# A gated recurrence with two products behind it: first products in pairs of blocks, and an opening that runs the recurrence ahead

## The chip, the cores and the metric

The kernel runs on one core of a Trainium2 chip. The metric is the device time of one execution in microseconds (us). The runs of the kernel before gave 195.75, 196.1 and 196.6 us, so the median is 196.1. One execution was also recorded by the hardware profiler, with all instructions of the engines: TensorE (PE, with its weight loads as PEld), VectorE (DVE), ScalarE (ACT), GpSimd (POOL) and SyncE (SP), which issues most transfers.

## The reference

```python
B, H, S, D = 4, 8, 768, 48
for t in range(S):
    state = alpha[:, :, t, :, None] * state + np.einsum('bhd,bhe->bhde', k[:, :, t], v[:, :, t])
    y[:, :, t] = np.einsum('bhd,bhde->bhe', q[:, :, t], state)
x = y.transpose(0, 2, 1, 3).reshape(B * S, H * D)      # 3072 x 384
h = x @ w_in                                           # 384 x 2048
r = np.maximum(h, 0.0)
g = s * (r * r) + b
out = g @ w_out                                        # 2048 x 384
```

For each of the 4 x 8 heads a state of 48 x 48 decays by alpha and takes in k and v, step by step in time; q reads it. The 8 heads of a step side by side are a row of 384, which goes through two matrix products with a squared Relu between them.

## The kernel before, in words

The 3072 rows are 24 blocks of 128 steps, six to each of the four sequences. For a block n the recurrence is computed in chunk form. In the order of its parts, with the names in the code:

- `load(n)`: four transfers of 192 KB each (alpha, k, q, v) into rings of eight buffers, issued by SP.
- `ln(n)`: ACT takes the logarithm of alpha. `vcast(n)`: POOL casts v.
- `cum(n)`: PE sums the logarithms over time (L210, for the first five blocks also the totals, L213) into the bank ct_ps; ACT takes exp(-) and exp(+) of it, bi_sb and b_sb (L221, L222). From the sixth block on, `decay(n)` writes the last row of b_sb to memory and reads it back transposed into blast, on SP (L230, L232); the second transfer waits for the landing of the first. The last block of a sequence has none.
- `qk(n)`: DVE multiplies k by bi_sb and q by b_sb (L238, L239). `tr(n)`: eight PE transposes into ct_ps (L244), copied by DVE to qkT (L249).
- `amat(n)`: eight small products q.k (L259) into the two banks a_ps, masked by DVE into am_a and am_b (L267).
- `y(n)`: products with the state of the block before and with the masked scores into y_ps (L278, L287), the products for the new state (L298), ACT's copy to y_bf (L305), and the new state by DVE (t_sb, L334) and POOL (L339, L343).
- `xt(n)`: three PE transposes of y_bf into an h_ps bank (L312), copied by ACT into xd_all (L318).

Behind it stand the two products. `m(n, u)`, u from 0 to 3, is a unit of the first: it fills one bank h_ps of 512 columns with four groups of three products of 128 columns (L365), ACT takes the Relu into r_sb (L379), DVE squares it into gt_all (L386). Two banks h_ps alternate, and xt uses them too. `o(n, u)`, u from 0 to 3, is a quarter of the second: four products of 384 columns (L402) into o_ps, or for blocks 1 and 2 into the two a_ps (`o_in_a`). After the last quarter the bank is evicted: for blocks 0 to 13 by ACT into room that the cast of w_in has freed (`keep_sb`, L411), for later ones by DVE with the bias (L415) and a store. `last(u)` is the second product of block 23, in two halves of 192 columns (L425).

Nothing schedules this at run time. Every engine runs its instructions in the order in which the program issues them, and the program sorts a list of events by a hand-given position. The opening, blocks 0 to 3 and part of 4, is one list written out (position 0.1 times its index). There w_in is cast while it lands (`win`), w_out in four parts (`wout`: parts 0, 1 and 3 by DVE in whole or in part, 2 by ACT), the column sums of w_out for the bias are built (`colsum`), and `busy` puts filler products. Behind it a block takes eight units of position: for block n, p = 8n is where y(n) stands; ln, cum, qk, tr, amat come up to 16.7 units ahead of it, xt one unit after, m(n, u) at p + 2.5 to 7.5 and o(n, u) at p + 8.5 to 14.5. `load(n + 5)` stands at p - 2.5. `GROUPS` gives how many blocks share a first product; here it is one for all.

Of the kernel before, what the change touches and what calls it, by code (L numbers as in the profile page):

```python
# [10 lines left out]
AF = mybir.ActivationFunctionType  # L11
# [3 lines left out]
def kernel(  # L15
# [12 lines left out]
    nc = tc.nc  # L28

    B, H, S, D = q.shape  # L30
    C = 128
    NCH = S // C
    NP = H // 2
    NBLK = B * NCH
    d_model = moe_w_in.shape[0]
# [1 line left out]
    NJ = d_ff // 128  # L37
    KT = d_model // 128

    GROUPS = [1] * NBLK  # L40
    UNITS = 5
    assert sum(GROUPS) == NBLK
    NLD = 8

# [10 lines left out]
    a_ps = [ps.tile([128, NP, 128], FP32, name=f"a_ps{i}") for i in range(2)]  # L55
    y_ps = ps.tile([128, 512], FP32, name="y_ps")
# [6 lines left out]
    def ring(name, shape, dtype, n):  # L63
        return [sb.tile(shape, dtype, name=f"{name}{i}") for i in range(n)]
# [29 lines left out]
    out_sb = ring("out_sb", [128, d_model], FP32, 3)  # L94
    xd_all = sb.tile([128, UNITS, KT * C], BF16, name="xd_all")
    gt_all = sb.tile([128, UNITS, NJ * C], BF16, name="gt_all")
    xd_sb, gt_sb, first_block = [], [], []
    for g, sz in enumerate(GROUPS):
        first_block.append(sum(GROUPS[:g]))
        u0 = first_block[g] % UNITS  # L100
        xd_sb.append(xd_all[:, u0 : u0 + sz].rearrange("a u x -> a (u x)").rearrange("a (t s) -> a t s", t=KT))
# [10 lines left out]
    NKEEP = 14  # L112
    keep_all = w_in_st.rearrange("a t f -> a (t f)")
    keep_sb = [keep_all[:, d_model * n : d_model * (n + 1)] for n in range(NKEEP)]
# [154 lines left out]
    group_of = []  # L269
    for g, sz in enumerate(GROUPS):  # L270
        group_of += [(g, i) for i in range(sz)]
# [82 lines left out]
    def mp(g, u):  # L354
        N = GROUPS[g] * C
        per = 512 // N
        if (g, u) in h_in_o:
            hp = o_ps
        else:
            hp = h_ps[nrelu[0] % 2]  # L360
            nrelu[0] += 1
        for jj in range(per):
            j = u * per + jj
            for kk in range(KT):
                nc.tensor.matmul(  # L365
                    out=hp[:, jj * N : (jj + 1) * N],
                    lhsT=w_in_bf[:, kk, 128 * j : 128 * (j + 1)],
                    rhs=xd_sb[g][:, kk, 0:N],
                    start=(kk == 0),
                    stop=(kk == KT - 1),  # L370
                )
        h_of[(g, u)] = hp
# [18 lines left out]

    o_in_a = {1: 0, 2: 1}

    def mm2(g, t, u):
        if g == NBLK - 1:
            return last(u)
        N = GROUPS[g] * C
        op = o_ps
        if g in o_in_a:
            op = a_ps[o_in_a[g]].rearrange("a p t -> a (p t)")  # L400
        for j in range(4 * u, 4 * u + 4):
            nc.tensor.matmul(  # L402
                out=op[:, 0:d_model],
                lhsT=gt_sb[g][:, j * N + t * C : j * N + (t + 1) * C],
                rhs=w_out_bf[:, j, :],
                start=(j == 0),
                stop=(j == NJ - 1),
            )
        if u == 3:
            if g < NKEEP:  # L410
                nc.scalar.activation(out=keep_sb[g], in_=op[:, 0:d_model], func=AF.Copy)  # L411
                return
            ot = out_sb[nout[0] % 3]
            nout[0] += 1
            nc.vector.tensor_tensor(out=ot, in0=op[:, 0:d_model], in1=bias_w, op=ALU.add)  # L415
            store(g, ot)


    def last(u):
        op = a_ps[0].rearrange("a p t -> a (p t)"), a_ps[1].rearrange("a p t -> a (p t)")  # L420
        hc = d_model // 2
        for half, j0, j1 in ((0, 0, 8), (1, 0, 8), (0, 8, 16), (1, 8, 16))[u : u + 1]:
            cols = slice(half * hc, half * hc + hc)
            for j in range(j0, j1):
                nc.tensor.matmul(  # L425
                    out=op[half][:, 0:hc],
                    lhsT=gt_sb[NBLK - 1][:, j * C : (j + 1) * C],
                    rhs=w_out_bf[:, j, cols],
                    start=(j == 0),
                    stop=(j == NJ - 1),  # L430
                )
            if j1 == NJ:
                ot = out_sb[(nout[0] + half) % 3]
                nc.vector.tensor_tensor(out=ot[:, 0:hc], in0=op[half][:, 0:hc], in1=bias_w[:, cols], op=ALU.add)
                nc.sync.dma_start(out=out[(NBLK - 1) * C : NBLK * C, cols], in_=ot[:, 0:hc])

    def store(n, o):
        nc.sync.dma_start(out=out[n * C : (n + 1) * C, :], in_=o)
# [39 lines left out]
    def at(pos, fn, *args):  # L478
        events.append((pos, len(events), fn, args))
# [26 lines left out]
        rl(g, u)  # L506

    def o(n, u):
        mm2(n, 0, u)


    for pos, what in enumerate(
        [
            (ln, 0), (vcast, 0), (cum, 0), (qk, 0), (spread,), (busy, 3), (tr, 0), (busy, 1), (ln, 1), (vcast, 1), (amat, 0),
            (cum, 1), (early, 2), (busy, 3), (yp, 0), (qk, 1), (st, 0), (busy, 1), (tr, 1), (xt, 0), (busy, 2), (amat, 1),
            (win, 0), (win, 1), (busy, 5), (yp, 1), (ln, 2), (mr, 0, 0), (st, 1), (busy, 1), (xt, 1), (early, 3), (cum, 2),
            (mr, 0, 1), (sq, 0, 0), (mr, 1, 0), (vcast, 2), (qk, 2), (mr, 1, 1), (busy, 1), (sq, 0, 1), (tr, 2), (win, 2),
            (busy, 3), (amat, 2), (sq, 1, 0), (busy, 3), (mr, 0, 2), (yp, 2), (win, 3), (st, 2), (mr, 1, 2), (xt, 2),
            (mp, 0, 3), (ln, 3), (rl, 0, 3), (mp, 1, 3), (cum, 3), (rl, 1, 3), (sq, 1, 1), (mr, 2, 0), (vcast, 3), (sq, 0, 2),
            (qk, 3), (mr, 2, 1), (sq, 1, 2), (mr, 2, 2), (sq, 0, 3), (tr, 3), (wout, 0), (mr, 2, 3), (amat, 3), (sq, 1, 3),  # L520
            (o, 0, 0), (busy, 3, y_ps), (sq, 2, 0), (yp, 3), (st, 3), (sq, 2, 1), (sq, 2, 2), (sq, 2, 3), (wout, 1), (o, 1, 0), (xt, 3),
            (o, 2, 0), (m, 3, 0), (m, 3, 1), (wout, 2), (o, 0, 1), (o, 1, 1), (colsum, 1), (ln, 4), (m, 3, 2), (m, 3, 3),
            (wout, 3), (o, 2, 1), (cum, 4), (o, 0, 2), (vcast, 4), (qk, 4), (o, 1, 2), (o, 2, 2), (colsum, 2), (o, 0, 3),
            (o, 1, 3), (o, 2, 3), (tr, 4), (o, 3, 0), (amat, 4),
        ]
    ):
        at(0.1 * pos, *what)
# [7 lines left out]
    for n in range(NKEEP):  # L535
        at(125.3 + 4.55 * n, add_bias, n)
        at(126.2 + 4.55 * n, store, n, keep_sb[n])
    for u in range(1, 4):
        at((30.5, 31.2, 32.5)[u - 1], o, 3, u)
    at(20.0, load, NLD)  # L540
    for n in range(4, NBLK):
        p = 8 * n
        if n > 4:
            f = min((n - 5) / 3.0, 1.0)
            c, t, a = 9.0 + 5.8 * f, 5.8 + 5.0 * f, 3.4 + 4.5 * f
            at(p - c - 1.9, ln, n)
            at(p - c + 0.01, vcast, n)
            at(p - c, cum, n)
            at(p - c + 0.2, qk, n)
            at(p - t, tr, n)  # L550
            at(p - a, amat, n)
        at(p, y, n)
        if n + 5 < NBLK:
            at(p - 2.5, load, n + NLD - 3)
        for u in range(4):
            at(p + (2.5, 3.5, 5.5, 7.5)[u], m, n, u)
            at(p + (8.5, 9.5, 12.5, 14.5)[u], o, n, u)
        at(p + 1.0, xt, n)
    for _, _, fn, args in sorted(events, key=lambda e: e[:2]):
        fn(*args)  # L560

# [29 lines left out]
```

## Time and profile before

| | |
|---|---|
| median of three runs | 196.1 us |
| the profiled execution's own time | 195.75 us |
| its span, first to last instruction | 194.0 us |
| granted TensorE clock | 1.00 throughout |
| PE busy from 0 to 10, 10 to 20, 20 to 30 us | 5.17, 8.57, 9.48 us |
| PE busy from 30 to 40, 40 to 50, 50 to 60 us | 9.75, 9.79, 8.97 us |
| PE busy from 70 to 140 us | 10.00 of each 10 us |
| share of the 16 DMA engines, 0 to 60 us | nearly full |
| DMA, mean over the span | 156 GB/s |

A line of the timeline or of the groups names an engine, a line of the program, an operation, what it writes and reads, and how many instructions it merges; a bracket at its end is the time for which the engine was idle before it, and whose work ended that. The record of a PE instruction is longer than its share of the engine, since products follow each other before the one ahead has drained: where the spacing of starts matters, the starts are compared. The chain of waits is followed back from the end, and names at each moment what the end hung on.

### The profile page before, as it was taken

What the parts mean: (1) busy time and instruction counts of PE and PEld (TensorE: products, weight loads), DVE (VectorE), ACT (ScalarE), POOL (GpSimd) and SP (SyncE); (2) the same over time, 40 slices, a digit from 0 to 9 for tenths busy, and PEclk for the clock granted to TensorE, in tenths of its full rate; (3) what the DMA queues carried; (4) which work ended last, traced back from release to release, by engine and by line L of the source; (5) the groups of instructions that cost most, each with busy time, mean ns of one, the idle gap of its engine ahead of it and who ended that gap; (6) DMA issues with size and microseconds to landing.
All of it is one profiled execution on the core that took longest, in us unless ns stands there. A gap on an engine that the chain in (4) does not pass through costs nothing.

```text
span 194.0 us, 6099 instructions
## 1 busy us (share of the span) xinstructions
PE 182.6 (94%) x2435; PEld 145.1 (75%) x2438; DVE 151.8 (78%) x296; ACT 118.7 (61%) x244; POOL 63.8 (33%) x96
## 2 busy tenths in 40 slices
PE   0997999999889999999999999999999999999994
PEld 0564696775767778878887888888877877887783
DVE  5466779986588787888977996878988999998632
ACT  3344777565667666677586676775676666654640
POOL 6153132611310514453600651552401474362000
PEclk9999999999999999999999999999999999999999
DMA  7999999899999847855978569649849584323212
GB/s 124 189 331 222 335 256 373 212 199 189 178 197 134 140 71 122 156 98 81 203 126 147 95 91 163 115 81 176 204 94 194 118 175 141 109 83 124 82 44 81
DMA packets 113454, 30.33 MB, mean 156 GB/s; under 512 B 106627, under 2 KB 111890, under 8 KB 113426
## 3 DMA queue, kind: packets, MB, share of 16 engines
q1 hardware_dynamic: 109262, 29.15, 74.6%
q10 hardware_dynamic: 4164, 0.79, 2.9%
q8 instruction: 19, 0.31, 0.7%
q14 instruction: 9, 0.07, 0.1%
HBM read 25.19 MB, written 4.74 MB: 154 GB/s over the span
## 4 chain that ended last, share of the span: by engine, by line
PE 81%; DMA 5%; SPq 4%; ACT 4%; DVE 3%; issue 1%; ACTq 0%; DVEq 0%
PE h_ps L365 30%; PE o_ps L402 28%; PE ct_ps L244 5%; DMA al_sb<-in_alpha_dram 5%; PE a_ps L259 4%; PE a_ps L402 3%; PE y_ps L287 2%; PE h_ps L312 2%; PE ct_ps L210 2%; ACT r_sb L379 2%; PE p_ps L298 2%; PE y_ps L278 2%; PE a_ps L425 1%; DVE qkT L249 1%; SPq L131 1%
## 5 line engine op out<-in xcount | busy, mean ns | idle before, releaser
L379 ACT ACTIVATE r_sb<-h_ps 128x512 bf16<-128x512 f32 x94 | 55.7, 597 | 37.4 <-PE h_ps L365 35.9
L365 PE MATMUL h_ps<-xd_all,w_in_bf 128*128 128x128 bf16 x1128 | 74.7, 219 | 0.7 <-ACT xd_all L318 0.3
L365 PEld LDWEIGHTS <-w_in_bf 128*128 128x128 bf16 x1152 | 69.1, 98 | 7.6 <-issue 1.7
L402 PE MATMUL o_ps<-w_out_bf,gt_all 128*128 128x384 bf16 x336 | 68.5, 326 | 0.1
L386 DVE TENSOR_TENSOR gt_all<-r_sb 128x512 bf16<-128x512 bf16 x96 | 46.0, 493 | 24.9 <-ACT r_sb L379 24.3
L339 POOL TENSOR_TENSOR sd_sb<-t_sb,blast 48x192 bf16<-48x192 f32 x40 | 22.4, 561 | 95.9 <-DVE t_sb L334 50.7
L402 PEld LDWEIGHTS <-gt_all 128*128 128x128 bf16 x368 | 32.5, 98 | 15.9
L206 POOL CAST v_bf<-v_sb 128x384 bf16<-128x384 f32 x24 | 18.2, 765 | 16.7 <-DMA v_sb<-in_v_dram 16.4
L343 POOL TENSOR_TENSOR sc_sb<-t_sb,blast 112x384 f32<-112x384 f32 x16 | 20.9, 1308 | 1.3
L318 ACT ACTIVATE xd_all<-h_ps 128x384 bf16<-128x384 bf16 x24 | 11.8, 490 | 15.1 <-PE h_ps L312 15.1
L249 DVE COPY qkT<-ct_ps 112x1024 bf16<-112x1024 bf16 x24 | 16.4, 685 | 4.9 <-PE ct_ps L244 3.4
L238 DVE TENSOR_TENSOR kb_sb<-k_sb,bi_sb 128x384 bf16<-128x384 f32 x24 | 14.1, 586 | 5.5 <-ACT bi_sb L221 3.7
L267 DVE TENSOR_TENSOR am_a<-a_ps,mask 128x512 bf16<-128x512 f32 x24 | 16.4, 683 | 1.8 <-PE a_ps L259 1.8
L267 DVE TENSOR_TENSOR am_b<-a_ps,mask 128x512 bf16<-128x512 f32 x24 | 16.3, 681 | 0.0
L239 DVE TENSOR_TENSOR qb_sb<-q_sb,b_sb 128x384 bf16<-128x384 f32 x24 | 16.0, 668 | 0.0
L203 ACT ACTIVATE la_sb<-al_sb 128x384 bf16<-128x384 f32 x24 | 12.4, 517 | 5.1 <-DMA al_sb<-in_alpha_dram 5.1
L221 ACT ACTIVATE bi_sb<-ct_ps 128x384 f32<-128x384 f32 x24 | 11.7, 487 | 4.4 <-PE ct_ps L213 2.6
L210 PE MATMUL ct_ps<-la_sb,U_bf 128*128 128x384 bf16 x24 | 8.2, 340 | 5.8 <-ACT la_sb L203 5.8
L305 ACT ACTIVATE y_bf<-y_ps 128x384 bf16<-128x384 f32 x24 | 11.7, 488 | 2.8 <-PE y_ps L287 2.8
L222 ACT ACTIVATE b_sb<-ct_ps 128x384 f32<-128x384 f32 x24 | 11.8, 494 | 0.0
L244 PEld LDWEIGHTS <-qb_sb 128*112 128x112 bf16 x96 | 8.7, 136 | 3.9 <-DVE qb_sb L239 2.4
L259 PE MATMUL a_ps<-qkT 48*128 48x128 bf16 x192 | 9.7, 222 | 1.0 <-DVE qkT L249 0.8
(67 smaller groups left out, 193.8 us busy)
## 6 DMA issues: line engine op xcount, KB each, us to landing
al_sb<-in_alpha_dram SPq DMA_DIRECT2D x24, 192.0 KB
k_sb<-in_k_dram SPq DMA_DIRECT2D x24, 192.0 KB
q_sb<-in_q_dram SPq DMA_DIRECT2D x22, 192.0 KB
v_sb<-in_v_dram SPq DMA_DIRECT2D x22, 192.0 KB
w_in_st<-in_moe_w_in_dram SPq DMA_DIRECT2D x4, 768.0 KB
w_out_st<-in_moe_w_out_dram SPq DMA_DIRECT2D x4, 768.0 KB
out_dram<-w_in_st SPq DMA_DIRECT2D x14, 192.0 KB
out_dram<-out_sb SPq DMA_DIRECT2D x9, 192.0 KB
```

The lines of the kernel that those rows point to most:

```text
L206: nc.gpsimd.tensor_copy(out=v_bf[n % 3], in_=v_sb[n % NLD])
L239: nc.vector.tensor_tensor(out=qb_sb[n % 2][:, :, 0:48], in0=q_sb[n % NLD], in1=b_sb[n % 3], op=ALU.mult)
L244: nc.tensor.transpose(out=t_ps[0:112, x, p, :], in_=t.rearrange("a h d -> a (h d)")[:, 128 * p : 128 * p + 112], identity=ident,)
L249: nc.vector.tensor_copy(out=qkT_sb[n % 2][0:112].rearrange("a x p t -> a (x p t)"), in_=t_ps[0:112].rearrange("a x p t -> a (x p t)"),)
L259: nc.tensor.matmul(out=a_ps[e][:, p, :], lhsT=qkT[r0 : r0 + 48, 1, p, :], rhs=qkT[r0 : r0 + 48, 0, p, :], start=True, stop=True,)
L267: nc.vector.tensor_tensor(out=am_sb[e][n % 2], in0=a_ps[e], in1=mask4, op=ALU.mult)
L339: nc.gpsimd.tensor_tensor(out=sd[r, :, d], in0=t1_sb[r, :, d], in1=bl[r].to_broadcast([48, NP, 48]), op=ALU.mult)
L343: nc.gpsimd.tensor_tensor(out=sc_sb[0:112], in0=t1_sb[0:112], in1=bl[0:112].to_broadcast([112, NP, 96]), op=ALU.mult)
L365: nc.tensor.matmul(out=hp[:, jj * N : (jj + 1) * N], lhsT=w_in_bf[:, kk, 128 * j : 128 * (j + 1)], rhs=xd_sb[g][:, kk, 0:N], start=(kk == ...
L379: nc.scalar.activation(out=rs, in_=h_of.pop((g, u)), func=AF.Relu)
L386: nc.vector.tensor_tensor(out=gt_sb[g][:, u * 512 : (u + 1) * 512], in0=rs, in1=rs, op=ALU.mult)
L402: nc.tensor.matmul(out=op[:, 0:d_model], lhsT=gt_sb[g][:, j * N + t * C : j * N + (t + 1) * C], rhs=w_out_bf[:, j, :], start=(j == 0), sto ...
```

## The change

Three things change together.

- *Pairs.* Blocks 0 to 5 keep first products of their own; from block 6 on, two blocks share them (nine pairs). A unit of a pair fills one h_ps bank with two groups of three products of 256 columns, and a pair has eight units. The second products stay by block; they read gt_all by the pair's layout. xd_all and gt_all hold six blocks in place of five. Block 22's second products go to y_ps, and the halves of block 23 are done one after the other.
- *The opening.* Its list now goes on past block 4: it holds blocks 4 to 6 whole but for part of their second products, and the recurrence of blocks 7 and 8 as far as amat(7) and qk(8). The casts of w_out parts 1 and 2 now stand ahead of block 3's first units, the first column sum between those units and qk(4), and the second products of blocks 0 to 4 lie among the recurrence's parts.
- *Behind the opening.* y(n) stands at 8(n - 1), one block earlier than before, the rest of the recurrence with it. Loads are placed by three blocks ahead, in place of five; on SP the loads of blocks 8, 9 and 10 now each follow the decay transfers of blocks 6, 7 and 8.

```diff
-    GROUPS = [1] * NBLK
-    UNITS = 5
+    LONE = 6
+    GROUPS = [1] * LONE + [2] * ((NBLK - LONE) // 2)
+    UNITS = 6
...
-    def mm2(g, t, u):
-        if g == NBLK - 1:
+    def mm2(n, u):
+        if n == NBLK - 1:
             return last(u)
+        g, t = group_of[n]
         N = GROUPS[g] * C
         op = o_ps
-        if g in o_in_a:
-            op = a_ps[o_in_a[g]].rearrange("a p t -> a (p t)")
+        if n == NBLK - 2:
+            op = y_ps
+        if n in o_in_a:
+            op = a_ps[o_in_a[n]].rearrange("a p t -> a (p t)")
...
-        for half, j0, j1 in ((0, 0, 8), (1, 0, 8), (0, 8, 16), (1, 8, 16))[u : u + 1]:
+        for half, j0, j1 in ((0, 0, 8), (0, 8, 16), (1, 0, 8), (1, 8, 16))[u : u + 1]:
...
-            (o, 0, 0), (busy, 3, y_ps), (sq, 2, 0), (yp, 3), (st, 3), (sq, 2, 1), (sq, 2, 2), (sq, 2, 3), (wout, 1), (o, 1, 0), (xt, 3),
-            (o, 2, 0), (m, 3, 0), (m, 3, 1), (wout, 2), (o, 0, 1), (o, 1, 1), (colsum, 1), (ln, 4), (m, 3, 2), (m, 3, 3),
-            (wout, 3), (o, 2, 1), (cum, 4), (o, 0, 2), (vcast, 4), (qk, 4), (o, 1, 2), (o, 2, 2), (colsum, 2), (o, 0, 3),
-            (o, 1, 3), (o, 2, 3), (tr, 4), (o, 3, 0), (amat, 4),
+            (o, 0, 0), (busy, 3, y_ps), (sq, 2, 0), (yp, 3), (st, 3), (sq, 2, 1), (sq, 2, 2), (sq, 2, 3), (o, 1, 0), (xt, 3),
+            (o, 2, 0), (wout, 1), (wout, 2), (m, 3, 0), (m, 3, 1), (ln, 4), (wout, 3), (o, 1, 1), (o, 2, 1), (cum, 4),
+            (m, 3, 2), (m, 3, 3), (vcast, 4), (colsum, 1), (qk, 4), (o, 1, 2), (o, 2, 2), (tr, 4), (o, 1, 3), (ln, 5), (o, 2, 3),
+            (amat, 4), (cum, 5), (o, 0, 1), (vcast, 5), (qk, 5), (o, 0, 2), (y, 4), (o, 0, 3), (xt, 4), (m, 4, 0),
+            (tr, 5), (m, 4, 1), (ln, 6), (o, 3, 0), (amat, 5), (cum, 6), (load, 8), (m, 4, 2), (vcast, 6), (qk, 6), (o, 3, 1),
+            (m, 4, 3), (y, 5), (o, 3, 2), (xt, 5), (tr, 6), (o, 3, 3), (ln, 7), (m, 5, 0), (amat, 6), (cum, 7), (load, 9),
+            (m, 5, 1), (vcast, 7), (qk, 7), (o, 4, 0), (m, 5, 2), (y, 6), (m, 5, 3), (xt, 6), (tr, 7), (o, 4, 1), (ln, 8),
+            (o, 4, 2), (amat, 7), (cum, 8), (load, 10), (colsum, 2), (o, 4, 3), (vcast, 8), (qk, 8), (o, 5, 0),
...
-    for u in range(1, 4):
-        at((30.5, 31.2, 32.5)[u - 1], o, 3, u)
-    at(20.0, load, NLD)
-    for n in range(4, NBLK):
-        p = 8 * n
-        if n > 4:
-            f = min((n - 5) / 3.0, 1.0)
-            c, t, a = 9.0 + 5.8 * f, 5.8 + 5.0 * f, 3.4 + 4.5 * f
+    for n in range(LONE + 1, NBLK):
+        p = 8 * (n - 1)
+        if n > 8:
+            c, t, a = (13.2, 10.4, 7.9) if n == 9 else (14.8, 10.8, 7.9)
...
+        elif n == 8:
+            at(p - 6.7, tr, n)
+            at(p - 4.4, amat, n)
         at(p, y, n)
-        if n + 5 < NBLK:
-            at(p - 2.5, load, n + NLD - 3)
-        for u in range(4):
-            at(p + (2.5, 3.5, 5.5, 7.5)[u], m, n, u)
-            at(p + (8.5, 9.5, 12.5, 14.5)[u], o, n, u)
+        if n == 9:
+            at(p - 12.2, load, 11)
+        if n > 8 and n + 3 < NBLK:
+            at(p - 12.1, load, n + 3)
         at(p + 1.0, xt, n)
+    for u in range(1, 4):
+        at(8 * LONE + (0.5, 1.5, 4.5)[u - 1], o, LONE - 1, u)
+    for n in range(LONE, NBLK, 2):
+        p, g = 8 * n, group_of[n][0]
+        for u in range(8):
+            at(p + (2.5, 3.5, 5.5, 7.5, 10.5, 11.5, 13.5, 15.5)[u], m, g, u)
+            d = (12.5, 14.5, 16.5, 17.5, 20.5, 22.5, 24.5, 25.5)[u]
+            if n == NBLK - 4 and u > 5:
+                d = 31.6 + 0.1 * (u - 6)
+            elif n == NBLK - 2 and u < 2:
+                d = (9.5, 12.5)[u]
+            at(p + d, o, n + u // 4, u % 4)
```

More of the change, by code (lines that the diff above doesn't have):

```diff
@@ L409, in mm2 @@
         if u == 3:
-            if g < NKEEP:
-                nc.scalar.activation(out=keep_sb[g], in_=op[:, 0:d_model], func=AF.Copy)
+            if n < NKEEP:
+                nc.scalar.activation(out=keep_sb[n], in_=op[:, 0:d_model], func=AF.Copy)
                 return
@@ L415, in mm2 @@
             nc.vector.tensor_tensor(out=ot, in0=op[:, 0:d_model], in1=bias_w, op=ALU.add)
-            store(g, ot)
+            store(n, ot)
     def last(u):
@@ L421, in last @@
         hc = d_model // 2
-        for half, j0, j1 in ((0, 0, 8), (1, 0, 8), (0, 8, 16), (1, 8, 16))[u : u + 1]:
+        g, t = group_of[NBLK - 1]
+        N = GROUPS[g] * C
+        for half, j0, j1 in ((0, 0, 8), (0, 8, 16), (1, 0, 8), (1, 8, 16))[u : u + 1]:
             cols = slice(half * hc, half * hc + hc)
@@ L426, in last @@
                     out=op[half][:, 0:hc],
-                    lhsT=gt_sb[NBLK - 1][:, j * C : (j + 1) * C],
+                    lhsT=gt_sb[g][:, j * N + t * C : j * N + (t + 1) * C],
                     rhs=w_out_bf[:, j, cols],
@@ L508, in o @@
     def o(n, u):
-        mm2(n, 0, u)
+        mm2(n, u)
     for pos, what in enumerate(
```

## The prediction

> **What bounds the kernel now.** I read the page first: TensorE (PE) is busy nearly all the span. Then the chain of waits in order of time, which says where another engine ends last.
>
> ```profile
> span 194.0 us, 6099 instructions
> ...
> PE 182.6 (94%) x2435; PEld 145.1 (75%) x2438; DVE 151.8 (78%) x296; ACT 118.7 (61%) x244; POOL 63.8 (33%) x96
> ...
> L365 PE MATMUL h_ps<-xd_all,w_in_bf 128*128 128x128 bf16 x1128 | 74.7, 219 | 0.7 <-ACT xd_all L318 0.3
> ```
> ```profile
> 79.62 1.34 PE h_ps L365 x24
> 80.96 0.65 PE o_ps L402 x4
> ...
> 86.66 1.34 PE h_ps L365 x24
> ...
> 188.47 2.65 PE a_ps L425 x32
> ```
>
> Columns of the chain: start, length, what. From 64 us to the last product the chain is PE alone but for one place at 139.5, one block each 7.04 us (79.62 to 86.66). The lengths give the true price of a product when they follow each other: 24 of 128 columns in 1.34 us, 55.8 ns each; 4 of 384 in 0.65, 163 ns; 32 of 192 in 2.65, 83 ns. The table of busy time by stretches shows PE busy 10.00 of each 10.00 us from 70 to 140. The only holes left there are the two of 0.10 and 0.12 us about each block's score products (L259), and the change keeps those. So two things can move the time: fewer nanoseconds of PE work, or PE waits, and these lie before 66 us. The next view, the timeline of single engines, shows one of them and the pace of the helpers:
>
> ```profile
> 49.74 0.49 ACT L411 ACTIVATE w_in_st<-o_ps 128x384 f32<-128x384 f32 x1 [0.33 <-PE o_ps L402]
> 50.13 0.48 ACT L318 ACTIVATE xd_all<-h_ps 128x384 bf16<-128x384 bf16 x1
> ```
> ```profile
> 49.55 0.33 PE L312 MATMUL h_ps<-ident,y_bf 128*128 128x128 bf16 x3
> 49.71 0.39 PE L244 MATMUL ct_ps<-ident,qb_sb 128*112 128x128 bf16 x4
> 49.94 0.39 PE L244 MATMUL ct_ps<-ident,kb_sb 128*112 128x128 bf16 x4
> 50.67 1.50 PE L365 MATMUL h_ps<-xd_all,w_in_bf 128*128 128x128 bf16 x24 [0.34 <-ACT xd_all L318]
> ```
>
> Read: block 4's transposed rows leave PE at 49.72 (3 of 0.056), ACT is still evicting another block (49.74, next start 0.39 later), copies xd_all until 50.61, and the first product starts at 50.67. Eight transposes (0.45 us) fill part of the hole; 0.51 us of it remain.
>
> I summed all PE starts from 34.46 us (the last instruction before the two orders part) to 65.4 us against the spacing of each kind: PE waits **2.7 us** there (0.2 at 37, 0.4 at 46, 0.5 at 50, 0.35 at 52, 0.45 at 54, 0.4 at 55, 0.4 in three after 61). That is all that a better order there could win.
>
> **The change, part by part.**
>
> *Wider first products.* Blocks 6 to 23 have 18 x 48 = 864 products of 128 columns (L365); they become 432 of 256. No row has 256 columns; between 83 ns at 192 and 163 at 384 a straight line gives 83 + 64 x 80/192 = 109.7 ns, against 2 x 55.8 = 111.6. Gain 1.9 ns x 432 = 0.8 us; with the per-product overhead read from 192 to 384 (163 - 2 x 83 = -3 ns for one product saved) 1.3. I take 1.05, ends 0 and 1.3. The 432 weight loads that go (98 ns each as recorded) are hidden already: with one before every product the spacing is 55.8. Relus (L379) and squares (L386) keep count and shape.
>
> [...]
>
> *The opening's new order.* I walked the changed order by hand, each engine in its own order, from 34.46 us with these rows. PE's last column to the start on ACT or DVE: 0.20 to 0.27 us (xd_all above; relu 51.59 after products that end at 51.34); ACT or DVE to PE 0.06. Start to start, back to back: ACT relu 0.50, Ln 0.41, Exp 0.38, evictions 0.39, the w_out cast 1.46; DVE square 0.33, kb and qb 0.47 each, mask product 0.60 each, qkT copy 0.60, column sum 0.87. In the walk PE waits at:
> 1. cum of block 4, 0.8 us. The ACT cast of w_out now stands ahead of block 3's first two relus and block 4's Ln; Ln can't start before alpha lands, which I place at 39.1 (it ran at 39.60 before, straight behind the cast; q of block 4, two loads later at 1.05 us each, had landed by 41.0). PE is through its two second products at 38.85, cum at 39.65. Ends 0.3 and 1.3.
> 2. tr of block 4, **1.9 us**. On DVE, qk(4) now stands behind two squares of block 3 and the first column sum, whose products follow cum: cum 39.65, Exps on ACT until 41.1, relus 41.1 and 41.6, squares until 42.58, sum until 43.45, kb, qb until 44.47. PE has only two products and two second products to do, until 42.63. Before, cum stood behind those products and six second products behind qk.
> 3. amat of block 4, **0.9 us**. It writes the two banks from which ACT must first evict blocks 1 and 2 (o_in_a); their last products now come just ahead, with Ln(5) between the two evictions: o(2,3) ends 46.27, eviction until 47.11, amat 47.17.
> 4. the first product of block 4, **1.0 us**: xt then directly m, the quoted hole without the transposes, 0.51 + 0.45.
> 5. amat(5) 0.2, cum(6) 0.1, xt(5) 0.3, cum(7) 0.15, xt(6) 0.25: 1.0 in all, behind DVE and ACT as before.
> 6. o(5,0) straight behind o(4,3) in the same bank, **0.9 us**: the last column, 0.2, Exps in front 0.1, eviction 0.49, 0.06.
>
> With 0.25 that both orders have at 35.9 and 37.4: 6.7 us against 2.7, **+4.0**. The opening's list then ends at 68.35.
>
> *Behind it.* The first units of the pair have few second products among them (the blocks' own come 10 to 12 places later than their first products), and DVE has a backlog: y(8) waits 0.3 for its mask product, amat(9) 0.4 for qkT, tr(10) 0.1: **+0.8**, ends 0 and 1.5. From about 80 us PE is full again, with as many instructions per block on ACT and DVE as before, so nothing is caught up.
>
> *Loads.* SyncE (SP) is the queue that loads are moved past:
>
> ```profile
> 49.84 1.75 SPq L131 DMA_DIRECT2D v_sb<-in_v_dram  x1
> ...
> 58.30 0.95 SPq L131 DMA_DIRECT2D v_sb<-in_v_dram  x1
> 59.34 0.74 SPq L230 DMA_DIRECT2D row_dr<-b_sb  x1
> 62.49 0.82 SPq L232 DMA_DIRECT2D blast<-row_dr  x2
> 63.37 0.44 SPq L122 DMA_DIRECT2D al_sb<-in_alpha_dram  x1
> ```
>
> Loads to block 7 are out at 51.6. Before, blocks 8 and 9 went out at once; now each of 8, 9, 10 stands behind a row of decays, on whose landing SP waits (L232): row, 1.5 to 3.1 us, the two blasts 0.85, four loads 2.7, some 7 us in all, a block's time. Rows wait for b_sb: b(6) at 55.7, so load 8 at 58.1, 9 at 65, 10 at 72, alpha landing 3.2 later. By the walk Ln(8) is due at 64.7, Ln(9) at 69.3, Ln(10) at 74.8 against 61.3, 68.2, 75.4; Ln(11) about a microsecond early too. Relus already ahead and products of y and amat on PE cover that much: 0, at worst 3 us if each row takes the 3.1. After the sequence's last block, which has no row, SP gains 4 us and is ahead.
>
> *Tail.* The last pair's eight units lie among second products of blocks 20 to 22, and the last 32 products are the same 2.65 us: 0, ends -0.3 and +0.5.
>
> **Sum** against the profiled execution (195.75 us, span 194.0): +4.0 + 0.8 - 1.05 = +3.75, so 199.5, span 197.75. The median of the runs is 196.1, 0.35 above that execution; from it 199.9, the number I give.
>
> **Rivals.**
> - *Half the waits.* Engines run closer together than my walk lets them, and half of what it adds stays: 2.4 - 1.05 = +1.35, 197.4. For it: small waits of 0.1 to 0.3 may be latencies twice counted. Against: items 2, 3, 4 and 6, 4.7 us, follow from one engine's order or one bank.
> - *The backlog works*, on the other side: with blocks 5 to 8 ready early PE finds its operands, the old 2.7 us go and nothing new comes; 1.05 + 2.7 = 3.75 gained, 192.3; with half the old waits left 193.7. It decides once the added waits come to less than 1.05 us, that is if items 2 and 3 are not there. For it: operands of blocks 5 to 7 land at 46, 50 and 55, ahead of need. Against: DVE's order in item 2.
> - *The change does little*: waits come out as before, only the width is left, 195.0.
> - *Loads late*: the SP chain above at 3.1 us a row and with ACT held by Ln, +3 more: 202.9. For it the spacing of 7 us; against, 0.6 us of lateness under 1.5 of cover.
>
> **Chances.** Forecast 0.52 (198.3 to 201.5), half the waits 0.18, the backlog works 0.14, little 0.07, loads late 0.09. What a measurement can tell from no change is about 0.5%, 1.0 us: faster by more 0.17 (the backlog, and part of "little"), within 0.08 (the rest of it and a little of the halves), slower 0.75. The range 195.6 to 202.0 leaves out the faster cases and most of the late loads.
>
> **What would show it.** In the changed profile: 24 columns' worth of first products (12 instructions of 256) in 1.31 us; PE waits of 1.9 us before block 4's transposes near 43, 0.9 before its scores near 46, 1.0 before its first product near 50, 0.9 after o(4,3) near 67; PE full from 80 on; Ln of blocks 10 and 11 released by DMA. Wrong if those four waits come to under 2 us, if 256 columns take much less than 109 ns, or if a wait on loads stands in the chain after 75.

## The result and the profile after

The changed kernel takes 203.58 us (median of six runs, 202.81 to 204.05) against 195.93 for the kernel before (six runs): a ratio of 1.0388, 95% interval 1.0362 to 1.0414. It was forecast slower at 199.9; the loss is 7.65 us where 3.75 was forecast, and the time lies above the range.

In some executions of either kernel the mean granted TensorE clock is recorded at 0.99 or 0.98, which in the profiled execution of the changed kernel (0.992) is one stretch of 3.41 us at a half; three of the six executions of the changed kernel show it, and at full clock it takes 202.8 to 203.4 us where the kernel before takes 195.2 to 196.1 in most of its executions, so 7.3 us of the loss do not hang on that.

The page of the changed kernel, its groups with shapes kept apart, and the group of second products on the page of the kernel before:

```profile
span 202.0 us, 5230 instructions
...
PE 182.5 (90%) x2003; PEld 138.7 (69%) x2006; DVE 149.9 (74%) x296; ACT 117.7 (58%) x244; POOL 60.4 (30%) x96
```
```profile
L407 PE MATMUL o_ps<-w_out_bf,gt_all 128*128 128x384 bf16 x320 | 64.7, 326 | 4.4 <-DVE out_sb L420 3.7 <-ACT w_in_st L416 0.7
...
L367 PE MATMUL h_ps<-xd_all,w_in_bf 128*128 128x256 bf16 x432 | 56.0, 273 | 0.0
```
```profile
L402 PE MATMUL o_ps<-w_out_bf,gt_all 128*128 128x384 bf16 x336 | 68.5, 326 | 0.1
```

(The lines moved: what was L365 is now L367, L402 is L407, L415 is L420, L238 and L239 are L240 and L241, L244 is L246, L259 is L261.) PE has 432 products fewer and is busy as long as before, 182.5 us in a span 8 us longer. The last numbers of the groups of second products tell what is new: PE was idle ahead of them for 0.1 us before and is for 4.4 us now, 3.7 of it until DVE has evicted o_ps.

Busy time hides waits of products that overlap: one of 384 columns is recorded at 326 ns, and back to back the next starts 162.5 ns behind it. So I laid the starts of PE's instructions against the spacing that each kind has back to back (56 ns for 128 columns, 109 for 256, 162.5 for 384) and called the rest waits; the price is the sum of these spacings. In the changed kernel's stretch of half clock 128 columns start 107 ns apart instead of 56, and the surplus counts as waiting here. Both profiled executions are cut at the same places of the second products' order:

| PE waits, us | before | after | more | forecast |
|---|---|---|---|---|
| start to o(1,0) | 9.28 | 10.14 | +0.86 | 0 |
| to o(5,1): the opening's list | 3.32 | 6.49 | +3.17 | +4.0 |
| to o(7,0): behind it | 0.65 | 1.68 | +1.03 | +0.8 |
| to o(14,1) | 1.56 | 1.71 | +0.15 | 0 |
| to the last product | 2.23 | 6.10 | +3.87 | 0 |
| price of PE's products | 169.50 | 168.46 | -1.04 | -1.05 |

The sum is +8.04, the spans differ by 8.03. The price came out as worked, the list 0.8 us below and the stretch behind it 0.2 above the forecast. Two rows were not in the forecast at all: the late waits, and 0.86 us in a stretch whose order did not change.

**The opening, as walked.** The timeline of the changed kernel around its largest hole (start, length, engine and line, idle before and who ended it):

```profile
41.18 1.15 ACT L381 ACTIVATE r_sb<-h_ps 128x512 bf16<-128x512 f32 x2
41.53 1.46 PE L407 MATMUL a_ps<-w_out_bf,gt_all 128*128 128x384 bf16 x8
41.83 1.07 DVE L388 TENSOR_TENSOR gt_all<-r_sb 128x512 bf16<-128x512 bf16 x2 [0.66 <-ACT r_sb L381]
42.82 0.95 DVE L177 TENSOR_TENSOR cs_sb<-w_out_st 128x768 f32<-128x768 f32 x1
43.69 0.55 DVE L240 TENSOR_TENSOR kb_sb<-k_sb,bi_sb 128x384 bf16<-128x384 f32 x1
44.16 0.55 DVE L241 TENSOR_TENSOR qb_sb<-q_sb,b_sb 128x384 bf16<-128x384 f32 x1
44.76 0.43 PE L246 MATMUL ct_ps<-ident,qb_sb 128*112 128x128 bf16 x4 [1.76 <-DVE qb_sb L241]
```

DVE does two squares and the column sum before kb and qb; PE has issued its last second product (eight from 41.53, 1.30 us of starts) by 42.83 and starts the transposes at 44.76: 1.92 us, forecast 1.9.

**The late waits.** The same view where DVE evicts block 14 and PE then starts block 15's second products, and who waited for whom in the whole execution:

```profile
140.76 1.47 PE L367 MATMUL h_ps<-xd_all,w_in_bf 128*128 128x256 bf16 x12
140.90 0.50 ACT L224 ACTIVATE b_sb<-ct_ps 128x384 f32<-128x384 f32 x1
141.05 0.56 DVE L240 TENSOR_TENSOR kb_sb<-k_sb,bi_sb 128x384 bf16<-128x384 f32 x1 [0.22 <-ACT bi_sb L223]
141.53 0.55 DVE L241 TENSOR_TENSOR qb_sb<-q_sb,b_sb 128x384 bf16<-128x384 f32 x1
142.00 0.55 DVE L420 TENSOR_TENSOR out_sb<-o_ps,bias_w 128x384 f32<-128x384 f32 x1
142.60 0.81 PE L407 MATMUL o_ps<-w_out_bf,gt_all 128*128 128x384 bf16 x4 [0.37 <-DVE out_sb L420]
```
```profile
PE o_ps L407 <- DVE out_sb L420: 3.7, 5, 1.0
```

A block's last quarter of second products now stands 1.5 units into the eight of a block, just behind cum and qk of a block to come. From block 14 on DVE evicts o_ps, and on DVE the eviction (142.00) stands behind kb and qb; here kb waits 0.22 us for ACT's Exp (L223), at the four later evictions DVE comes to kb from other work without a pause. PE has two units of first products for cover, 1.31 us. Before, the quarter stood 6.5 units in, and DVE evicted 3 us ahead of kb:

```profile
133.38 0.55 DVE L415 TENSOR_TENSOR out_sb<-o_ps,bias_w 128x384 f32<-128x384 f32 x1
134.44 0.82 PE L402 MATMUL o_ps<-w_out_bf,gt_all 128*128 128x384 bf16 x4
136.38 0.56 DVE L238 TENSOR_TENSOR kb_sb<-k_sb,bi_sb 128x384 bf16<-128x384 f32 x1
136.85 0.86 DVE L239 TENSOR_TENSOR qb_sb<-q_sb,b_sb 128x384 bf16<-128x384 f32 x1
```

There are five such waits, of 0.53, 0.68, 1.16, 0.98 and 1.16 us by the starts, and five is the number of blocks from 14 on that still have a later block's qk beside their last quarter. In the two of 1.16 us something adds to DVE's queue:

```profile
156.16 1.13 POOL L345 TENSOR_TENSOR sc_sb<-t_sb,blast 112x384 f32<-112x384 f32 x1
156.52 1.18 DVE L241 TENSOR_TENSOR qb_sb<-q_sb,b_sb 128x384 bf16<-128x384 f32 x1
```

Here, and again at 172.61, qb takes 1.11 us from its start to the next one in place of 0.47, while POOL's sc_sb runs. That is 0.64 us of each of the two waits; no run tests POOL's part by itself.

### The profile page after: what moved, and what is told of

Its sections match the earlier page's. It is cut to its first block, busy times and chain, and to the rows that moved or that the text cites. A ratio compares the mean times of both kernels' runs of the same rounds, so it can differ in the third digit from the quotient of the medians.

```text
span 202.0 us, 5230 instructions
## 1 busy us (share of the span) xinstructions
PE 182.5 (90%) x2003; PEld 138.7 (69%) x2006; DVE 149.9 (74%) x296; ACT 117.7 (58%) x244; POOL 60.4 (30%) x96
## 4 chain that ended last, share of the span: by engine, by line
PE 67%; DVE 9%; DMA 9%; ACT 6%; SPq 4%; issue 3%; DVEq 0%; ACTq 0%
PE h_ps L367 25%; PE o_ps L407 22%; DMA al_sb<-in_alpha_dram 6%; PE ct_ps L246 5%; PE a_ps L261 3%; DVE qb_sb L241 2%; ACT r_sb L381 2%; PE ct_ps L212 2%; PE a_ps L407 2%; PE h_ps L314 2%; PE y_ps L289 2%; DMA row_dr<-b_sb 1%; PE a_ps L432 1%; PE y_ps L407 1%; DVE am_a L269 1%
## 5 line engine op out<-in xcount | busy, mean ns | idle before, releaser
L367 PE MATMUL h_ps<-xd_all,w_in_bf 128*128 128x256 bf16 (+1 forms) x696 | 75.2, 256 | 1.0 <-ACT xd_all L320 0.8
L407 PE MATMUL o_ps<-w_out_bf,gt_all 128*128 128x384 bf16 x320 | 64.7, 326 | 4.4 <-DVE out_sb L420 3.7
L367 PEld LDWEIGHTS <-w_in_bf 128*128 128x128 bf16 x720 | 60.2, 100 | 11.1 <-issue 1.5
L388 DVE TENSOR_TENSOR gt_all<-r_sb 128x512 bf16<-128x512 bf16 x96 | 42.9, 461 | 29.6 <-ACT r_sb L381 29.0
L341 POOL TENSOR_TENSOR sd_sb<-t_sb,blast 48x192 bf16<-48x192 f32 x40 | 21.9, 547 | 100.6 <-DVE t_sb L336 60.9
L407 PEld LDWEIGHTS <-gt_all 128*128 128x128 bf16 x368 | 33.9, 98 | 22.0 <-issue 5.5
L208 POOL CAST v_bf<-v_sb 128x384 bf16<-128x384 f32 x24 | 17.1, 713 | 17.1 <-DMA v_sb<-in_v_dram 13.4
L251 DVE COPY qkT<-ct_ps 112x1024 bf16<-112x1024 bf16 x24 | 16.5, 687 | 6.3 <-PE ct_ps L246 6.1
L345 POOL TENSOR_TENSOR sc_sb<-t_sb,blast 112x384 f32<-112x384 f32 x16 | 19.2, 1201 | 1.3
L320 ACT ACTIVATE xd_all<-h_ps 128x384 bf16<-128x384 bf16 x24 | 11.8, 490 | 12.6 <-PE h_ps L314 12.5
L241 DVE TENSOR_TENSOR qb_sb<-q_sb,b_sb 128x384 bf16<-128x384 f32 x24 | 17.9, 747 | 0.0
L240 DVE TENSOR_TENSOR kb_sb<-k_sb,bi_sb 128x384 bf16<-128x384 f32 x24 | 13.7, 572 | 5.1 <-ACT bi_sb L223 5.1
L269 DVE TENSOR_TENSOR am_b<-a_ps,mask 128x512 bf16<-128x512 f32 x24 | 16.3, 681 | 0.0
L223 ACT ACTIVATE bi_sb<-ct_ps 128x384 f32<-128x384 f32 x24 | 11.7, 488 | 5.6 <-PE ct_ps L212 2.5
L246 PEld LDWEIGHTS <-qb_sb 128*112 128x112 bf16 x96 | 8.2, 133 | 5.5 <-DVE qb_sb L241 4.6
L246 PE MATMUL ct_ps<-ident,qb_sb 128*112 128x128 bf16 x96 | 9.8, 226 | 2.2 <-DVE qb_sb L241 2.2
```

The source lines that it names most:

```text
L208: nc.gpsimd.tensor_copy(out=v_bf[n % 3], in_=v_sb[n % NLD])
L240: nc.vector.tensor_tensor(out=kb_sb[n % 3][:, :, 0:48], in0=k_sb[n % NLD], in1=bi_sb[n % 2], op=ALU.mult)
L241: nc.vector.tensor_tensor(out=qb_sb[n % 2][:, :, 0:48], in0=q_sb[n % NLD], in1=b_sb[n % 3], op=ALU.mult)
L246: nc.tensor.transpose(out=t_ps[0:112, x, p, :], in_=t.rearrange("a h d -> a (h d)")[:, 128 * p : 128 * p + 112], identity=ident,)
L251: nc.vector.tensor_copy(out=qkT_sb[n % 2][0:112].rearrange("a x p t -> a (x p t)"), in_=t_ps[0:112].rearrange("a x p t -> a (x p t)"),)
L269: nc.vector.tensor_tensor(out=am_sb[e][n % 2], in0=a_ps[e], in1=mask4, op=ALU.mult)
```

## The experiments

The theory after the result: the opening's order costs 3.2 us and about 1 behind it; the late waits come from DVE's order around the eviction; pairs as such are cheap. Rivals, by their letters in the expectations: a ring of three out_sb that waits for stores (R), a chain of loads and decay rows on SP (S), pairs as such (P), gains given back later (G). All edits are to the changed kernel unless said.

**1. qk behind the eviction.**

```diff
-            at(p - c + 0.2, qk, n)
+            at(p - c + (0.4 if n > 18 else 0.2), qk, n)
```

> The changed kernel with one thing moved on DVE: from block 19 on, the kb and qb products (L240, L241) stand behind the eviction of o_ps by DVE (L420) instead of ahead of it. Theory E (DVE's order: the eviction queues behind kb and qb, which wait for ACT's Exps): the five waits of PE for o_ps between 140 and 175 us (0.53, 0.68, 1.16, 0.98, 1.16, together 4.5 us) go, and the time falls by 3.9 to 4.5 us to about 199.4. Theory R (ring: the eviction waits for a free one of the three out_sb, that is for stores on SP): the waits stay and so does the time, 203.6. Theory P (the pairs' rhythm starves PE there whatever evicts): the waits move to another line, time above 202.

Measured: 202.24 us, ratio 1.0328 (1.0260 to 1.0397). The waits for o_ps are gone, but only 1.8 of the 3.9 us of late waits with them (6.10 to 4.30). In their place PE waits for qb ahead of the transposes, 0.69, 0.51, 0.76 and 0.52 us:

```profile
149.28 0.81 PE L407 MATMUL o_ps<-w_out_bf,gt_all 128*128 128x384 bf16 x4
149.71 0.85 DVE L241 TENSOR_TENSOR qb_sb<-q_sb,b_sb 128x384 bf16<-128x384 f32 x1
150.62 0.43 PE L246 MATMUL ct_ps<-ident,qb_sb 128*112 128x128 bf16 x4 [0.53 <-DVE qb_sb L241]
```

Theory E as I had put it was half right: it is not which of the three goes first. Kb, qb and the eviction have to be done between the Exps and the transposes, and what goes last holds PE.

**2. Six output buffers.** `ring("out_sb", ..., 6)` in place of 3.

> The changed kernel with six out_sb buffers in place of three, nothing moved. Theory R: the five waits of PE for o_ps after 140 us go, about 199.4 us. Theory E: they stay, each within 0.2 us of its old size, and the time is 203 to 204 us.

Measured: one execution, 205.96 us. The late waits are 6.10 us, to the hundredth what they were: R falls. The time is longer for another reason, seen in the table of busy time by stretches (columns: stretch and length, busy time and number of PE, PEld, DVE, ACT and POOL, granted clock, DMA share, GB/s):

```profile
42.00:46.00 4.00, 2.06 (x14) 1.30 (x15) 2.58 (x4) 0.36 (x1) 0.13 (x1) 0.84 1.12 190
46.00:50.00 4.00, 3.64 (x18) 1.58 (x17) 1.93 (x4) 1.90 (x5) 0.51 (x1) 0.50 1.30 191
```

The granted clock is a half from 44.7 to 51.6 us, 0.85 us behind the end of the opening's largest hole, which is 2.12 us in this execution; the second products there start 0.32 us apart instead of 0.16, and the waits of that stretch, against full-clock spacing, are 9.4 us instead of 6.5.

**3. No pairs.** `GROUPS = [1] * NBLK`, with m and o of blocks 6 to 23 at the places of the kernel before; everything else as changed.

> The changed kernel without pairs: first products of one block each throughout, at the places where the kernel before had them (first products 2.5 to 7.5 and second products 8.5 to 14.5 units after 8n); opening, recurrence a block ahead, loads three ahead and six buffers of xd_all and gt_all stay. Theory O (the opening's order costs by itself 2.9 us in its list and about 1.2 behind it, the late waits belong to the pairs' places of second products): 195.9 + 4.1 = 200.0, perhaps 0.9 more if the first 35 us are slower again as in the profile of the change; no wait of PE for o_ps over 0.3 us after 140. Theory P (pairs carry the whole loss): 196 us. Theory L (the late waits come with the recurrence being a block ahead): they stay, 203 to 204.6 us.

Measured: 200.62 us, ratio 1.0225 (1.0176 to 1.0273). PE's waits are 6.50 in the list, 1.19 behind it, and then 1.56 and 2.21, as in the kernel before. So the order without pairs makes 4.7 us, and the late waits belong to the places of the pairs' second products, not to the recurrence being a block ahead.

**4. Loads first.** The entries (load, 8), (load, 9) and (load, 10) stand ahead of (amat, 4), and so ahead of block 6's decay transfers on SP.

> The changed kernel with the loads of blocks 8, 9 and 10 placed on SP ahead of the decay transfers of block 6, as the kernel before had blocks 8 and 9. Theory S (the serial SP chain of decay rows and loads holds PE behind the opening): the 1.7 us of PE waits between 67 and 84 us fall to 0.5, time 1 us less, 202.4. Theory D (those waits are DVE's backlog): they stay within 0.3 us, 203.2 to 203.9 us; the row of block 6, now behind twelve transfers, lands later and may add a wait of POOL that PE does not see.

Measured: 206.00 us, ratio 1.0505 (1.0448 to 1.0563). The waits behind the opening are 1.47 us instead of 1.68, where S said 0.5. The wait ahead of block 8's transposed rows falls from 0.28 us to 0.12, and the one ahead of block 10's transposes from 0.37 to 0.30. In the changed kernel's chain of waits both follow from block 10's Ln, which ACT starts 0.45 us late because alpha lands late; on SP that load stands behind block 8's decay row:

```profile
71.34 4.01 DMA al_sb<-in_alpha_dram
75.43 0.52 ACT la_sb L205
```

With the loads first Ln(10) does not wait; in experiments 1 and 2 it waits 0.69, and the stretch has 1.9 us of waits. The 0.56 us ahead of block 9's scores stay, and they end with DVE's qkT. So theory D holds for most of the stretch, and S for a small part. The row of block 6 did reach PE, which theory D had not expected: its landing behind twelve loads holds POOL's sd_sb, and y of block 7 starts 1.1 us late.

```profile
68.73 1.76 POOL L341 TENSOR_TENSOR sd_sb<-t_sb,blast 48x192 bf16<-48x192 f32 x2 [13.55 <-DMA blast<-row_dr]
70.54 0.33 PE L280 MATMUL y_ps<-sd_sb,qkT 112*128 112x96 bf16 x4 [0.96 <-POOL sd_sb L341]
```

The clock too was a half from 44.4 to 47.8 us in the profile, and all four executions have a mean clock below full, 0.983 to 0.992.

**5. The second products of blocks 14 to 23 later.**

```diff
             d = (12.5, 14.5, 16.5, 17.5, 20.5, 22.5, 24.5, 25.5)[u]
+            if n >= NKEEP:
+                d = (16.5, 17.5, 20.5, 22.5, 24.5, 25.5, 28.5, 30.5)[u]
```

> The changed kernel with the second products of the pairs from block 14 on (those that DVE evicts) two quarters later, so that a block's last quarter and its eviction stand 6.5 units into the eight of a block, where the kernel before had them, and no longer 1.5 units in, just behind cum and qk. Theory E2 (between the Exps and the transposes DVE has to do kb, qb and an eviction, and whichever goes last holds PE: moving qk behind the eviction only handed 2.5 of 4.5 us to the transposes): with the eviction elsewhere both waits go; PE's waits after 137 us fall from 6.1 to about 2.3, time 3.8 us less, 199.8. Theory P (the pairs' rhythm itself, 8 units of first products among them, starves PE): the waits stay above 4.5 us in sum, time above 202.

Measured: 200.86 us, ratio 1.0269 (1.0224 to 1.0315). PE's waits from o(14,1) on are 2.61 us instead of 6.10 (the stretch before has 0.4 more). Among executions with one stretch of half clock it takes 200.6 to 200.9 against 203.8 to 204.05: 3.2 us. So 3.1 of the 3.87 us hang on these places, what POOL adds there included, and theory P, that the pairs' rhythm itself starves PE, falls.

**6. qk of block 4 first.** `(cum, 4), (vcast, 4), (qk, 4), (m, 3, 2), (m, 3, 3), (colsum, 1)`.

> The changed kernel with one thing moved in the opening: qk of block 4 directly behind its cum, ahead of block 3's last two units and of the column sum. Theory O2 (DVE's order makes PE wait 1.9 us before block 4's transposes, and nothing later gives it back): that wait goes, PE's waits in the opening's list fall from 6.5 to 4.6 us, time 1.9 us less, 201.7, and more if the clock drops less often. Theory G (given back: the chain of block 4 and 5 waits elsewhere, at its scores or at y): under 0.7 us gained, above 202.9.

Measured: 201.02 us, ratio 1.0297 (1.0239 to 1.0356). PE's waits in the list are 4.52 us instead of 6.49, at full clock 200.7 to 201.1 us against 202.8 to 203.4: 2.0 us, nothing given back. The transposes follow the second products without a hole, the waits of block 4's scores and first product stay:

```profile
40.55 1.46 PE L407 MATMUL a_ps<-w_out_bf,gt_all 128*128 128x384 bf16 x8
41.85 0.39 PE L246 MATMUL ct_ps<-ident,qb_sb 128*112 128x128 bf16 x4
...
44.48 0.38 PE L261 MATMUL a_ps<-qkT 48*128 48x128 bf16 x7 [0.56 <-ACT w_in_st L416]
...
48.58 0.83 PE L367 MATMUL h_ps<-xd_all,w_in_bf 128*128 128x128 bf16 x12 [0.79 <-ACT xd_all L320]
```

**7. Fillers in the holes.** `(busy, 8, y_ps)` before (tr, 4), 3 before (amat, 4), 4 before (m, 4, 0), 3 before (o, 5, 0).

> The changed kernel with 18 filler products of 512 columns (of which nothing is used) in the four holes of the opening, before block 4's transposes, scores and first product and before block 5's second products. Theory H (the holes let the granted clock drop to a half for one or two stretches of 3.4 us in some executions; the profiles of two variants showed it at 44 to 51 us): with PE busy the half clock appears in no execution between 40 and 60 us; times of the executions lie 0 to 1.5 us lower, 202.5 in the median, and their spread shrinks. Theory N (the clock drops are not the holes' doing): as many executions below 0.995 as in the changed kernel, same time, or up to 1 us more where a filler outlasts its hole.

Measured: 204.34 us, ratio 1.0432 (1.0388 to 1.0475); at full clock 203.2 to 204.0, some 0.7 us more than without, and three of six executions have a mean clock under 0.995 (0.991 and 0.992), as many as without fillers. In the one execution that was profiled the mean clock was 0.999. Theory H is not borne out, and not excluded either: only profiled executions show where a stretch lies.

**8. Three of the opening's holes.** Experiment 6, and (tr, 5) between (xt, 4) and (m, 4, 0), and o(5,0) at 48.1, behind y of block 7.

> The changed kernel with three of the opening's holes taken away: qk of block 4 directly behind its cum, block 5's transposes between block 4's xt and first product, and block 5's first quarter of second products behind y of block 7 and no longer straight behind the quarter that uses the same bank. Theory O2: 1.9 + 0.45 + 0.86 = 3.2 us less, 200.4; PE's waits in the list 3.3 us. Theory G (given back): less than half of it, above 202.

Measured: 201.12 us, ratio 1.0274 (1.0223 to 1.0325). PE's waits in the list are 3.67 us, 2.8 less, and at full clock it takes 200.3 and 200.5, 2.5 less. The list is then about where the kernel before had it (3.32).

**9. Both repairs, 5 and 8.**

> The changed kernel with both repairs: the opening's three holes taken away, and the second products of the pairs from block 14 on two quarters later. Theory A (the parts add: each repair's waits are its own): PE's waits are 3.7 in the list, 1.8 behind it and about 4.7 after 85 us, at full granted clock 202.9 - 2.7 - 3.1 = 197.1 us, still 0.6% above the kernel before. Theory G (one gives back what the other gains): above 198.5.

Measured: 198.18 us, ratio 1.0134 (1.0095 to 1.0173); the executions at full clock took 196.64, 197.16 and 197.59. The parts add: 197.1 was expected at full clock. PE's waits by the five rows of the table are 9.08, 3.70, 1.66, 2.12, 2.24. What is left against the kernel before is 0.4 in the list, 1.0 behind it and 0.6 from block 7's second products on, against 1.04 from the width.

**10. Pairs on the kernel before.** Its opening and its loads; the recurrence moves ahead by `min(max(n - 5, 0), 8)` units; `LONE = 14`, second products at 16.5 to 30.5 but for block 14's first two at 12.5 and 14.5.

> The kernel before with its own opening and its loads five ahead; the recurrence moves one unit of the order ahead per block from block 6 to 13 until it is a block ahead, and blocks 14 to 23 then go in five pairs, second products at the places of the repaired version. What the width gives: 240 products of 256 in place of 480 of 128, 0.58 us less PE work. Theory W (width gains what the rows say, the loss of the change was all in orders): 195.8 - 0.6 plus 0.2 to 0.8 of waits where the pairs begin, 195.3 to 196.1. Theory P (pairs cost by themselves): above 197.

Measured: 198.46 us, ratio 1.0154 (1.0122 to 1.0185). Opening and the stretch behind it are those of the kernel before (3.32 and 0.62), the price is 0.58 lower, and yet the later waits are 3.50 and 3.61 us against 1.56 and 2.23. By the time alone this is theory P (above 197). But the waits stand at places that this run's order makes, most of them where blocks have few second products between recurrence parts:

```profile
129.56 0.40 PE L260 MATMUL a_ps<-qkT 48*128 48x128 bf16 x8
129.74 0.49 ACT L306 ACTIVATE y_bf<-y_ps 128x384 bf16<-128x384 f32 x1
130.29 0.34 PE L313 MATMUL h_ps<-ident,y_bf 128*128 128x128 bf16 x3 [0.33 <-ACT y_bf L306]
```

Here xt stands directly behind amat (0.5 us of waiting by the starts), and twice m directly behind xt or cum (0.54 and 0.58). This run does not separate what pairs cost from its order; experiments 9 and 11 do that better.

**11. No pairs, and 8.**

> The changed kernel without pairs and with the opening's three holes taken away. Theory A (parts add): the run without pairs, 199.6 to 200.4 at full granted clock, less 2.7: 197.2; PE's waits 3.7 in the list, about 1.2 behind it and 3.8 after 84 us. Theory G: less than half of 2.7 is gained, above 198.5.

Measured: 198.08 us, 197.84 without the longest of the six executions, ratio 1.0102 (1.0068 to 1.0136). Waits 3.67, 1.81, 1.56, 2.22 from o(1,0) on: as expected, but behind the opening 0.6 more. With and without pairs the repaired order takes the same within the spread of the executions, 198.18 and 197.84. By the waits behind the list (6.02 and 5.59) pairs cost 0.4 of the 1.04 us that their width gives; what is left is too small for these runs to tell. No version that ran beats the kernel before.

## Why the prediction was wrong

Sign and mechanism of the opening were right; the range failed by a term of the sum that was put at nothing. Without that term the profiled sum comes near the forecast partly by luck: 0.8 us too much in the opening and 0.86 of half clock at the start nearly cancel.

- *Width*: forecast 1.05 us, measured 1.04; 256 columns start 109 ns apart. A weight load stands ahead of each product (720 for 720, recorded at 100 ns each) and does not show in the spacing.
- *The opening*: forecast +4.0, measured +3.2. Item 2 1.92 (1.9), item 3 0.75 plus the usual 0.1 (0.9), item 4 0.96 (1.0), item 6 0.86 (0.9). Item 1 was 0.16 instead of 0.8: block 4's Ln started at 39.29 straight behind ACT's relus, and in experiment 6, whose order to there is the same, already at 38.30, so alpha had landed earlier than the 39.1 at which I placed it. The small ones were 0.7 instead of 1.0. Experiments 6 and 8 showed that what is taken from these holes comes off the end.
- *Behind it*: forecast +0.8, measured +1.03. Most of it is DVE's, as I had it: 0.56 ahead of block 9's scores, 0.3 ahead of block 10's transposes. The loads, which I had put at nothing, have some 0.2 (experiment 4).
- *The step that failed*: "From about 80 us PE is full again, with as many instructions per block on ACT and DVE as before". I counted instructions and did not look at where they stand. The turn of the one bank o_ps had moved to the place in a block at which DVE has kb and qb to do, with 1.31 us of cover. I had worked this turn out for o(5,0) in the opening (item 6) and for o_ps nowhere else. It is 3.9 us where I had 0, and experiments 1, 3 and 5 pin it to DVE's work between Exps and transposes and to the places of the pairs' second products.
- *The start*: 0.86 us in the profiled execution, forecast 0. The order there is the same. The granted clock was a half from 18.9 to 22.3 us:

```profile
18.00:22.00 4.00, 3.28 (x32) 3.24 (x32) 1.79 (x4) 2.81 (x8) 1.74 (x3) 0.61 1.08 347
```

  It follows 2.2 us of waits between 16.3 and 18.7 us. Executions of the kernel before show a mean clock of 0.991 as well, and take 196.2 to 197.2 us then. In the profiles of experiments 2 and 4, whose order up to there is this one and whose clock did not fall there, o(1,0) starts at 34.33 and 34.60 us, against 35.35 here and 34.50 in the kernel before: it is a chance of the execution, not of the change. The clock of the kernel before was not full throughout, as the table ahead of the change has it: fillers of 512 columns start 0.427 us apart up to 11.2 us there and 0.216 from 14.5 us.
- *Rivals*: loads late, at +3, fell (experiment 4). Its sign did come, though: "a wait on loads stands in the chain after 75", 0.45 us ahead of block 10's Ln; block 11's did not wait. The backlog did not win back the old waits, and the waits did not come out at half.

## What to carry to other kernels

When an order is changed, follow every single-buffered bank through its turn: who evicts it, what stands ahead of the eviction on that engine, and how much work the producer has until it needs the bank; do it at each place in the period, also where the instruction counts did not change. Here a wait taken from one instruction by reordering a helper reappeared at the helper's next customer (experiment 1: the 4.5 us of waits for o_ps went, and the late waits fell by 1.8); move the work to where the helper is free instead (experiment 5: 6.10 us of late waits became 2.61). A walk by hand with back-to-back spacings, not mean durations, gave four of the six holes of a hand-written opening within a tenth or so; the one that hung on a landing was off by 0.6 us.

## What the runs showed of the hardware

The granted clock fell to a half (0.50) for stretches of 3.41 or 6.83 us: in the profiled executions of experiments 2 (44.7 to 51.6 us) and 4 (44.4 to 47.8) behind a wait of PE of 2.12 us, and once, between 18.7 and 23.2 us, in those of the changed kernel and of experiments 1, 5, 8 and 11, whose mean clocks are 0.990 to 0.992. In the trace of the changed kernel the clock is recorded full from 8.62 us, a half from 18.86 and full again from 22.27, so its changes lie 10.24 and 13.65 us behind the first, three and four times 3.41; in that of the kernel before it is recorded full from 13.55 us to the end. By the spacings, PE had waited 2.31 us of the 3.41 ahead of the fall at 18.86. In the same trace 1.96 us of waits between 42.75 and 46.16 had no fall behind them, and in the kernel before 1.75 between 15.8 and 19.2 had none. No run changes these waits alone, so what brings a fall is not shown.

The changed kernel's executions with a mean clock of 0.989 to 0.992 take 1.1 us more in the median than those at 0.998 to 1.00 (203.96 against 202.88), and in experiment 9 those at 0.990 and 0.991 take 1.8 more (198.92 against 197.16). Whether the opening's holes make such stretches more frequent is not settled by experiment 7. The traces point that way: of the six profiled executions with the hole of 1.9 us or more ahead of block 4's transposes two fell right behind it (experiments 2 and 4); of the seven without it five have a mean clock of 0.999 or 1.00, and in the other two (0.991, experiments 8 and 11) the stretch lies ahead of 24 us.

Where DVE's qb and POOL's sc_sb overlap, sc_sb is recorded longer, and in six of ten cases of the changed kernel qb too. Either qb is recorded at 1.18 us and sc_sb at 1.12 to 1.18, or qb at 0.55, as without POOL, and sc_sb at 1.58 to 2.24; the six sc_sb that no qb overlaps are recorded at 0.82 or 0.83.
